# Attention and a long convolution in one kernel: how the convolution's token operand is loaded

## The chip, the cores and the metric

The kernel runs on one core of a Trainium2 chip. The metric is the device time of one execution in microseconds (us). TensorE (PE) multiplies matrices, with its weight loads (PEld) beside them; VectorE (DVE), ScalarE (ACT) and GpSimd (POOL) work on elements; SyncE (SP) issues most of the DMAs. SBUF is the on-chip memory with 128 partitions, PSUM holds TensorE's results.

## What is computed

```python
B, S, D, H = 1, 2048, 448, 16        # Dh = 28, one key and value head
def _A_ref(x, wq, wk, wv, wo):       # attention
    q = (x @ wq).reshape(B, S, H, Dh).transpose(0, 2, 1, 3)
    k = x @ wk
    v = x @ wv
    p = softmax(einsum("bhqd,bkd->bhqk", q, k) * Dh ** -0.5)
    return einsum("bhqk,bkd->bhqd", p, v).transpose(0, 2, 1, 3).reshape(B, S, H * Dh) @ wo

def _B_ref(u, ...):                  # L = 2048 tokens, D = 448 channels, N = 256 modes
    P = exp(logdA[:, :, None] * l)                  # logdA = dt * A, complex
    K = einsum("dn,dnl,dn->dl", Cc, P, dB).real     # one filter of length L for each channel
    y = causal convolution of u with K, by channel  # written with FFTs of length 2 L
    return y + u * Dskip

g = sigmoid((x * gate_w).sum(-1, keepdims=True))
return g * a + (1 - g) * b           # a = _A_ref(x, ...), b = _B_ref(x, ...): u is x too
```

## The kernel before

Everything runs on one core in one program, and a planner orders it. The methods of the class `Kernel` only record operations: an engine, the code that emits the instruction, an estimated duration, the keys that it reads and writes, and a priority `pr`. `Prog.schedule` (a list scheduler, line 186) then goes through them in order of the earliest possible start by its own estimates, with the priority as second criterion, and so fixes one order of instructions for each engine. `emit` writes these orders out with semaphore waits. On the chip nothing is reordered: where an instruction waits longer than the planner thought, all that stands behind it on its engine is late. A DMA is issued from the queue of SyncE, ScalarE or GpSimd, in that engine's order. The planner also puts filler matmuls into gaps of TensorE.

**Attention** (`main`, line 1327). There are 1,024 tiles of 128 keys by 512 queries, in sets of three and two. For each set `qk` puts the scores into five PSUM banks of psS (line 1373 for the form of 29 rows with qT, line 1396 for the form of 128 rows with qM), and one ScalarE instruction takes the exponentials into a ring of 15 tiles, expT (line 1428). `pv` multiplies them with the values into psB (line 1449). After 64 tiles `norm` copies psB to acc (line 1173) on VectorE; the denominators take a round by DRAM (denT, R_scratch, rdenB) on GpSimd's queue. `qproj` makes the next queries (lines 893 to 905), and GpSimd's queue copies them to qM.

**Filters.** `masters` and `tables` build powers of the modes on VectorE (lines 934 to 1024), `kgen` multiplies them into the filters K (line 1047), 32 channels at a time, which go by kstg (line 1059) to the DRAM scratch KP.

**Convolution.** `tload` loads eight channels of K from KP as Toeplitz blocks (tile T, four DMAs on SyncE's queue). Buffers are used in turn: three in T (`NTR`), and late in the program two more in the room of U. `conv` multiplies, for each of 28 groups of 16 channels, with the token operand U as weights and T as the moving operand: for each of four groups of four channels, eight steps `n` of four matmuls that use the four column groups of the array (line 1114). Results go by lines 1124 and 1135 into O (line 1144), which gathers the output and starts as zeros.

**The token operand.** U holds half of the 448 channels (`UA` = 224). Partition 4r + h belongs to row r of a block of 32 tokens and to shift h; on each there are, for every channel, 64 numbers: 16 blocks of tokens for each of four groups i, where group i is zero on partitions with h < i and otherwise the tokens shifted by 512 (h - i). Two channels lie interleaved, so that the columns of one weight load are 4 numbers (8 B) apart. It is made in steps: the DMA zU fills U with zeros; 16 DMAs bring x into O as a staging place; `prep_u` (line 615) moves both halves of the channels with 32-bit copies on VectorE (line 627), the first into U and the second into the tile T at `UB`; 24 DMAs (`ushift`, line 606) copy group 0 with its shifts into the other groups, in pieces of 64 B; the DMA zO then fills O with zeros. Later, when the first half of the channels has been used, `ufill` (line 1091) fills U from T with the second half, seven DMAs for each of seven pieces, on GpSimd's queue.

The loads of this operand may not start before the third store of x (`self.late`). The shifts are written so:

```python
lst.append((bass.AP(tensor=self.U.h, offset=h * rs + do + 32 * i, ap=[[4 * rs, 32], [128, n // 2], [1, 32]]),
            bass.AP(tensor=src.h, offset=(h - i) * src.rs + so, ap=[[4 * src.rs, 32], [sd, n // 2], [1, 32]])))
```

Of the kernel before, what the change touches and what calls it, by code (L numbers as in the profile page):

```python
# [10 lines left out]
BF = mybir.dt.bfloat16  # L11
F32 = mybir.dt.float32
P = 128

S = 2048
D = 448
# [14 lines left out]
MC = 1280  # L31
NTR = 3
RING = 15
# [3 lines left out]
UA = D // 2  # L37
UB = 0
T0 = 16 * (D - UA)
TEND = 17280  # L40
XQ = NT * 512
QS = 4 * D + 64
# [386 lines left out]
class Kernel:  # L429
# [78 lines left out]
    def consts(self):  # L508
# [29 lines left out]
        for k, base in enumerate((-30, -31, -32)):  # L538
            ap = self.sel.v(0, 16, 128 * k, [[32, 4], [1, 32]])
            pm(ap, 1.0, 200, [("sel", k)], 3)  # L540
            pg.op("pool", lambda e, ap=ap, base=base: e.affine_select(
                out=ap, in_=ap, compare_op=ALU.is_equal, fill=0.0, base=base,
                pattern=[[0, 4], [1, 32]], channel_multiplier=2), 300, rd=[("sel", k)], wr=[("sel", k)], pr=3)
        dm(self.one.v(0, P, 0, [[1, 2]]), 1.0, 60, ["one"], 3)
        dm(self.one.v(0, P, 2, [[1, 2]]), 0.0, 60, ["one"], 3)

    def loads(self):
# [12 lines left out]
        def lraw(k, eng="sp"):  # L560
# [27 lines left out]
        Z = lambda n, r: self.cst.v(0, P, 512, [[0, r], [1, n // r]])  # L588
        uc = [("Uc", c) for c in range(14)]
# [15 lines left out]

    def ushift(self, dst, do, src, so, sd, n, r0):
        rs, ts = self.U.rs, self.T.rs
        lst = []
        for i in range(r0, 4):
            for h in range(i, 4):  # L610
                lst.append((bass.AP(tensor=self.U.h, offset=h * rs + do + 32 * i, ap=[[4 * rs, 32], [128, n // 2], [1, 32]]),
                            bass.AP(tensor=src.h, offset=(h - i) * src.rs + so, ap=[[4 * src.rs, 32], [sd, n // 2], [1, 32]])))
        return lst

    def prep_u(self):
        pg = self.pg
        done = []
        U4, T4, O4 = (b.cast(mybir.dt.int32) for b in (self.U, self.T, self.O))
        for half in range(2):
            for k in range(2):  # L620
                if half == 0:
                    dst, w = U4.v(0, P, 8 * k, [[64, UA // 2], [1, 8]]), ["Uz", ("Ub", k)]
                else:
                    dst, w = T4.v(0, P, UB // 2 + 8 * k, [[16, UA // 2], [1, 8]]), ["rawdone", ("UB", k)]
                key = ("ustd", half, k)
                done.append(key)
                pg.op("dve", lambda e, dst=dst, k=k, half=half: e.tensor_copy(
                    dst, O4.v(0, P, (8 * k * D + half * UA) // 2, [[1, UA // 2], [D // 2, 8]])), 1000,
                    rd=[("ust", k)] + ([] if half else []), wr=w + [key], pr=1 + half)
        for k, (c0, c1) in enumerate(((0, 2), (2, 5), (5, 9), (9, 14))):  # L630
            n = 16 * (c1 - c0)
            pg.dma(self.ushift(self.U, 1024 * c0, self.U, 1024 * c0, 128, n, 1), (6 * 16 * n, 64), f"du{k}", rd=[("Ub", 0), ("Ub", 1)],
                   wr=[("Uc", c) for c in range(c0, c1)], pr=0.35 if k < 2 else 0.9 + 0.1 * k, slow=True, iss=700.0)
        V0 = lambda b, off, n, r: b.v(0, P, off, [[n // r, r], [1, n // r]])
        Z = lambda n, r: self.cst.v(0, P, 512, [[0, r], [1, n // r]])
        pg.dma([(V0(self.O, 0, 16 * D, 32), Z(16 * D, 32))], (4096, 448), "zO", rd=[("cst", 1)] + done,
               wr=[(x, q) for q in range(16) for x in ("O", "Oz")], pr=1)

# [429 lines left out]
    def tbufs(self):  # L1068
        home = [(self.T, T0 + k * TW, 0) for k in range(NTR)] + [(self.U, 0, 42), (self.U, TW, 50)]
        last = [-1] * len(home)  # L1070
        self.tb = []
        for gi in range(56):
            s = min((k for k in range(len(home)) if gi >= home[k][2]), key=lambda k: last[k])
            self.tb.append((s, home[s][0], home[s][1], last[s] < 0))
            last[s] = gi

    def tload(self, gi):
        pg = self.pg
        s, buf, o, first = self.tb[gi]
        x = ["tpdone", "rawdone"] + ([("XS", 1)] if gi == NTR - 1 else []) if gi < NTR else []  # L1080
        w = [("T", s)]
        if first and s >= NTR:
            w += [("Uc", k) for k in range(o // 1024, (o + TW - 1) // 1024 + 1)]
# [7 lines left out]
    def ufill(self, c):  # L1091
        pg = self.pg
        lst = [(self.U.v(0, P, c * 2048, [[128, 16], [1, 32]]), self.T.v(0, P, UB + c * 512, [[32, 16], [1, 32]]))]
        lst += self.ushift(self.U, c * 2048, self.T, UB + c * 512, 32, 32, 1)
        for j, pair in enumerate(lst):
            pg.dma([pair], (2048 if j == 0 else 512, 64), f"uf{j % 4}", rd=[("UB", 0), ("UB", 1), ("yx", 2 * c + 5)],
                   wr=[("Uf", 2 * c, j), ("Uf", 2 * c + 1, j)], pr=1.2, slow=True, iss=1800.0 if j == 0 else 800.0, eng="pool", extra=3000)

    def conv(self, c):
# [4 lines left out]
        for k in range(4):  # L1104
# [5 lines left out]
            for n in range(8):  # L1110
                def mm(e, k=k, n=n, to=to, gi=gi, tbuf=tbuf):
                    m0, par = 2 * (n // 2), n % 2
                    for j in range(4):
                        r = e.matmul(ps.v(32 * j, 32 - m0, 128 * k, [[1, 128]]),  # L1114
                                     self.U.v(0, P, (4 * gi + j) % UA // 2 * 128 + 2 * (2 * m0 + par) + j % 2, [[4, 32 - m0]]),
                                     tbuf.v(0, P, to + j * TC + 32 * (13 - 2 * m0 - par), [[1, 128]]),
                                     start=(n == 0), stop=(n == 7), tile_position=(0, 32 * j), skip_group_check=True)
                    return r
                first = k == 0 and n == 0
                o = pg.op("pe", mm, 56, mode="c", ni=8, rd=[("T", s), ("Uc", c % 14), ("Ub", 0), ("Ub", 1)] + [("Uf", c % 14, j) for j in range(7)],  # L1120
                      wr=[X] + ([("cst", cs)] if first else []), pr=1.6,
# [79 lines left out]
    def scaled(self, half):  # L1201
# [4 lines left out]
        ov = self.onT.v(0, P, 512 * 3 + 256 * half, [[1, 256]])  # L1206
        dv = self.seedz.v(0, P, 8 * half, [[1, 8]])
        X, N = ("nx", half), ("dl", half)
# [21 lines left out]
        def m2(e):  # L1230
            for q in range(2):
                for h in range(4):
                    r = e.matmul(gv(32 * h, 32, 128 + 128 * q, [[1, 128]]), self.seedz.v(0, P, 8 * half + 4 * q + h, [[0, 32]]),
                                 self.dg(2 * half + q, [[1, P]]), start=True, stop=True, tile_position=(0, 32 * h), skip_group_check=True)
            return r
# [91 lines left out]
    def main(self):  # L1327
# [159 lines left out]
        for b, (c0, nb) in enumerate(BLOCKS):  # L1487
            self.masters(b)
            for c in range(c0, c0 + nb):
# [3 lines left out]
                self.conv(2 * c + 1)  # L1493
                if 2 <= c < 9:
                    self.ufill(c - 2)
        for a, b in HOLDC:
# [52 lines left out]
```

## Time and profile before

| | |
|---|---|
| three timed runs | 497.27, 497.94, 498.53 us (median 497.94) |
| span of the profiled execution, which is its own time | 498.8 us |
| first exponential starts, last one ends | 21.25 us, 491.98 us |
| busy: PE, DVE, ACT, POOL | 462.3, 458.6, 484.0, 183.8 us |
| granted TensorE clock, mean | 0.997 |
| DMA | 91.86 MB in 117,479 packets, mean 184 GB/s |

All comes from one execution. A group of instructions is named by its line, engine and operation, with the tile that it writes and those that it reads; a number in square brackets is the engine's idle time before it, with the instruction or DMA that ended it. Instructions of an engine overlap a little, so that the sum of their lengths can be more than its busy time.

### The profile page before, as it was taken

Reading aid. Unit: us, or ns where it says so; the run is one execution under the profiler, and the core shown is the slowest. Engines: PE = TensorE matmul, PEld = TensorE weight load, DVE = VectorE, ACT = ScalarE, POOL = GpSimd, SP = SyncE. Lnnn points to the kernel's source line nnn. Section 1 sums busy time; section 2 is a strip of 40 time slices with the busy share of each in tenths; the row PEclk is TensorE's granted clock in tenths of the full one; section 3 lists DMA queues with packets and bytes.
Section 4 is the critical chain, followed back from the end, with each engine's and each line's share of the span. In section 5 each row is a group of like instructions: output and inputs, shape, how many; then the busy total and the mean of one; then the engine's idle time right before and its main releaser. Section 6 shows DMA issues by size and latency. Waiting matters only on the chain.

```text
span 498.8 us, 17277 instructions
## 1 busy us (share of the span) xinstructions
PE 462.3 (93%) x7559; PEld 207.8 (42%) x7645; DVE 458.6 (92%) x872; ACT 484.0 (97%) x436; POOL 183.8 (37%) x331
## 2 busy tenths in 40 slices
PE   8899899999999999999999999999999999999997
PEld 5432233343443444444334344444534344444444
DVE  6998999999999999999999999999999999995224
ACT  6999899999999999999999999999999999999995
POOL 2102034225232527428616552643743525142110
PEclk9999899999999999999999999999999999999999
DMA  8996686935809555776942963798595695877752
GB/s 242 319 187 159 96 174 103 282 119 160 246 12 283 132 184 141 217 205 155 291 124 50 272 171 85 204 234 207 137 279 141 171 285 131 268 207 230 215 175 71
DMA packets 117479, 91.86 MB, mean 184 GB/s; under 512 B 48698, under 2 KB 112492, under 8 KB 117404
## 3 DMA queue, kind: packets, MB, share of 16 engines
q1 hardware_dynamic: 106746, 78.91, 57.7%
q0 software_dynamic: 10384, 11.70, 9.9%
q8 instruction: 60, 0.98, 0.9%
q10 hardware_dynamic: 274, 0.14, 0.1%
q14 instruction: 15, 0.12, 0.1%
HBM read 73.61 MB, written 5.23 MB: 158 GB/s over the span
## 4 chain that ended last, share of the span: by engine, by line
ACT 85%; SPq 6%; PE 4%; DVE 4%; DMA 1%; issue 0%
ACT expT L1428 84%; SPq L164 6%; DVE tab L988 1%; PE psS L658 1%; DMA O<-in_A_x_dram 1%; DVE tab L1003 0%; PE psS L1373 0%; PE psS L1396 0%; PE psS L1286 0%; PE psB L1349 0%; PE psB L1449 0%; ACT L805 0%; PE psS L1047 0%; DVE expT L680 0%; PE psX L1047 0%
## 5 line engine op out<-in xcount | busy, mean ns | idle before, releaser
L1428 ACT ACTIVATE expT<-psS 128x1536 bf16<-128x1536 f32 (+1 forms) x410 | 464.4, 1409 | 3.8 <-PE psS L1373 2.6
L988 DVE TENSOR_TENSOR tab<-tab,mbf 128x512 bf16<-128x512 bf16 (+4 forms) x140 | 139.4, 999 | 0.0
L1373 PE MATMUL psS<-qT,kT 29*128 29x512 bf16 x684 | 96.1, 386 | 12.0 <-ACT expT L1428 6.9
L1449 PE MATMUL psB<-expT,vaug 128*32 128x512 bf16 x1000 | 100.1, 390 | 2.2 <-DVE acc L1173 1.9
L1396 PE MATMUL psS<-qM,kT 128*128 128x512 bf16 x240 | 78.0, 382 | 13.8 <-issue 7.9
L164 POOL DMA_DIRECT2D KP_scratch<-kstg x104 | 57.1, 556 | 65.1 <-DVE kstg L1059 59.5
L1003 DVE TENSOR_TENSOR tab<-tab 128x256 bf16<-128x256 bf16 (+4 forms) x140 | 77.1, 571 | 0.0
L1449 PEld LDWEIGHTS psB<-expT,vaug 128*32 128x32 bf16 x1000 | 25.7, 93 | 74.9 <-issue 70.7
L164 POOL DMA_DIRECT2D qM<-qT x64 | 32.5, 516 | 59.0 <-DVE qT L905 38.4
L1373 PEld LDWEIGHTS psS<-qT,kT 29*128 29x128 bf16 x684 | 23.7, 91 | 64.3 <-ACT expT L1428 50.9
L164 POOL DMA_DIRECT2D U<-T x49 | 36.6, 750 | 36.2 <-DMA U<-T 14.6
L1355 PE MATMUL psB<-ident,one 128*128 128x512 bf16 x149 | 49.0, 389 | 0.0
L164 POOL DMA_DIRECT2D rdenB<-R_scratch x60 | 31.9, 538 | 34.6 <-DMA R_scratch<-denT 33.8
L1114 PE MATMUL psS<-T,U 128*26 128x128 bf16 (+3 forms) x1856 | 42.8, 221 | 0.5 <-issue 0.3
L1114 PEld LDWEIGHTS psS<-T,U 128*26 128x26 bf16 (+3 forms) x1856 | 32.9, 105 | 16.7 <-issue 11.7
L1017 DVE TENSOR_TENSOR tab<-tab,tmp 128x1984 bf16<-128x1984 bf16 x28 | 32.5, 1185 | 0.1
L1114 PE MATMUL psX<-T,U 128*32 128x128 bf16 (+3 forms) x1408 | 31.6, 221 | 0.0
L1396 PEld LDWEIGHTS psS<-qM,kT 128*128 128x128 bf16 x316 | 19.0, 97 | 30.1 <-ACT expT L1428 20.5
L164 POOL DMA_DIRECT2D denT<-acc x15 | 10.7, 716 | 55.8 <-DVE acc L1173 55.8
L1114 PEld LDWEIGHTS psX<-T,U 128*32 128x32 bf16 (+3 forms) x1408 | 24.3, 105 | 11.0 <-issue 7.4
L1011 DVE TENSOR_TENSOR tmp<-tmp,mq 128x64 bf16<-128x64 bf16 (+4 forms) x70 | 25.2, 360 | 0.0
L934 DVE TENSOR_TENSOR msq<-seedz 128x512 f32<-128x512 f32 (+1 forms) x40 | 24.6, 616 | 0.0
(188 smaller groups left out, 502.9 us busy)
## 6 DMA issues: line engine op xcount, KB each, us to landing
T<-KP_scratch SPq DMA_DIRECT2D x204, 272.0 KB, 4.9
U<-KP_scratch SPq DMA_DIRECT2D x20, 272.0 KB, 6.2
rdenB<-R_scratch POOLq DMA_DIRECT2D x60, 64.0 KB, 3.6
U<-cst SPq DMA_DIRECT2D x1, 3584.0 KB, 25.2
qM<-qT POOLq DMA_DIRECT2D x64, 32.0 KB, 3.7
tab<-in_A_x_dram SPq DMA_DIRECT2D x4, 448.0 KB, 5.3
O<-in_A_x_dram SPq DMA_DIRECT2D x16, 112.0 KB, 3.0
O<-cst SPq DMA_DIRECT2D x1, 1792.0 KB, 9.3
```

The source lines that it names most:

```text
L164: return [e.dma_start(o, i, **kw) for o, i in pairs]
L934: pg.op("dve", lambda e: e.tensor_tensor(m2(msq), z2, z2, ALU.mult), el(2 * n), rd=[kr, ki] + first, wr=["msq"], pr=pr)
L988: mul = lambda e, o, a, b: e.tensor_tensor(o, a, b, ALU.mult)
L1003: vo(lambda e, dv=dv, tv=tv, k=k: e.tensor_tensor(dv, dv, tv, ALU.add if k else ALU.subtract), n, [kt[k], kd[k]], [kd[k]], 1.92 if lv else ...
L1011: vo(lambda e, w=w, lv=lv: e.tensor_tensor(rho.v(0, P, (32 - 2 * w) * 2, [[64, 32], [2, w], [1, 2]]), rho.v(0, P, (32 - w) * 2, [[64, 32], ...
L1017: vo(lambda e, k=k: e.tensor_tensor(tab.v(0, P, FM + k * FP + 2, [[64, 32], [2, 31], [1, 2]]), tab.v(0, P, lm + k * PL + 62, [[64, 32], [- ...
L1114: r = e.matmul(ps.v(32 * j, 32 - m0, 128 * k, [[1, 128]]), self.U.v(0, P, (4 * gi + j) % UA // 2 * 128 + 2 * (2 * m0 + par) + j % 2, [[4, ...
L1355: return e.matmul(t.v(0, P, off, [[1, 512]]), self.one.v(0, P, 2, [[0, P]]), self.ident.v(0, P, 0, [[0, 4], [1, P]]), start=b != 6, stop=b ...
L1373: r = e.matmul(self.psS.v(0, P, 512 * b, [[1, 512]]), kT.v(32 * h, DH + 1, 128 * kt, [[1, 128]]), qT.v(32 * h, DH + 1, 512 * (i % 2), [[1, ...
L1396: return e.matmul(self.psS.v(0, P, 512 * b, [[1, 512]]), kT.v(0, P, 128 * kt, [[1, 128]]), self.qM.v(0, P, (i % 2) * XQ + 512 * h, [[1, 51 ...
L1428: o = pg.op("act", lambda e: e.activation(expT.v(0, P, 512 * es[0], spread(es, n)), self.psS.v(0, P, 512 * bs[0], spread(bs, n)), AF.Exp, ...
L1449: r = e.matmul(self.psB.v(32 * h, 32, 0, [[1, 512]]), vaug.v(0, P, 32 * kt, [[1, 32]]), expT.v(0, P, 512 * ring[t], [[1, 512]]), start=(kt ...
```

## The change

U gets another layout: two halves of 112 channels (`UC`), and in each 64 rows of 112 numbers, one for each group and block of tokens. The columns of a weight load are 2 `UC` = 224 numbers (448 B) apart. `uparts` loads every group and shift straight from x in DRAM, in pieces of 224 B: for each of the two halves four DMAs of group 0 and six of groups 1 to 3, on SyncE's queue. The staging in O, the 32-bit copies, the shift copies and the second half in T are gone. U's groups 1 to 3 and O become zero by 20 memsets of GpSimd instead of by DMA. `ufill` loads the second 224 channels from DRAM too, ten DMAs for each of six pieces (`FILLS`), in runs of 64 or 96 B, still on GpSimd's queue. The room that the second half had in T goes to a fourth Toeplitz buffer, and of the two late ones in U one remains. The end of that fourth buffer lies over the first part of the seeds (`seedz`), which moves into T; its first load waits for them.

```diff
-NTR = 3
+NTR = 4
...
-UB = 0
-T0 = 16 * (D - UA)
+UC = UA // 2
+UW = 64 * UC
+T0 = 0
...
+FILLS = ((0, 2), (2, 4), (4, 7), (7, 9), (9, 11), (11, 14))
...
-            self.prep_u()
...
-        self.T = sb("T", TEND, BF)
+        self.T = sb("T", TEND + 4 * W2, BF)
...
-        self.seedz = sb("seedz", 2 * W2, F32)
+        self.seedz = Sub(self.T.cast(F32), TEND // 2)
...
+        U4, O4 = (b.cast(mybir.dt.int32) for b in (self.U, self.O))
+        for b in range(2):
+            for k in range(6):
+                pm(V(U4, (b * UW + 16 * UC) // 2 + 448 * k, 448), 0, 470, [("Uz", b)], 4 + b)
+        for k in range(8):
+            pm(V(O4, 448 * k, 448), 0, 470, [(x, q) for q in (2 * k, 2 * k + 1) for x in ("O", "Oz")], 6)
...
-        self.late.append(pg.dma([(V0(self.U, 0, 64 * UA, 64), Z(64 * UA, 64))], (8192, 448), "zU", rd=[("cst", 1)],
-                                wr=["Uz"], pr=0.25).i)
-        for k in range(2):
-            lst = [(self.O.v(0, P, (8 * k + j) * D, [[1, D]]),
-                    dram(x, 32 * (15 - 8 * k - j) * D, [[D, 32], [512 * D, 4], [1, D]])) for j in range(8)]
-            self.late.append(pg.dma(lst, (1024, 896), f"u{k}", wr=[("ust", k)], pr=0.3).i)
+        self.x = x
+        for b in range(2):
+            for k, i0 in ((0, 0), (1, 1)):
+                lst = self.uparts(UC * b, UC * b, UC, (0, 1) if k == 0 else (1, 4))
+                o = pg.dma(lst, (512 * len(lst), 2 * UC), f"u{b}{k}", rd=[("Uz", b)] if k else [],
+                           wr=[("Uc", c) for c in range(7 * b, 7 * b + 7)] if k else [("Ub", b)], pr=0.3 + 0.6 * b)
+                self.late.append(o.i)
...
+    def uparts(self, dc, sc, n, groups):
+        rs = self.U.rs
         lst = []
+        for i in range(*groups):
             for h in range(i, 4):
+                lst.append((bass.AP(tensor=self.U.h, offset=h * rs + dc // UC * UW + 16 * i * UC + dc % UC,
+                                    ap=[[4 * rs, 32], [UC, 16], [1, n]]),
+                            dram(self.x, (512 * (h - i) + 480) * D + sc, [[D, 32], [-32 * D, 16], [1, n]])))
         return lst
...
-        home = [(self.T, T0 + k * TW, 0) for k in range(NTR)] + [(self.U, 0, 42), (self.U, TW, 50)]
+        home = [(self.T, T0 + k * TW, 0) for k in range(NTR)] + [(self.U, 0, 42)]
...
-        w = [("T", s)]
+        w = [("T", s)] + ([("zr", 0)] if first and o + TW > TEND else [])
...
+    def ufill(self, k):
         pg = self.pg
+        c0, c1 = FILLS[k]
+        n = 16 * (c1 - c0)
+        for j, pair in enumerate(self.uparts(16 * c0, UA + 16 * c0, n, (0, 4))):
+            pg.dma([pair], (512, 2 * n), f"uf{j % 4}", rd=[("yx", c1 + 3)],
+                   wr=[("Uf", c, j) for c in range(c0, c1)], pr=1.2, iss=800.0, eng="pool", extra=3000)
...
-                                     self.U.v(0, P, (4 * gi + j) % UA // 2 * 128 + 2 * (2 * m0 + par) + j % 2, [[4, 32 - m0]]),
+                                     self.U.v(0, P, (4 * gi + j) % UA // UC * UW + (2 * m0 + par) * UC + (4 * gi + j) % UC, [[2 * UC, 32 - m0]]),
```

More of the change, by code (lines that the diff above doesn't have):

```diff
@@ L615, in prep_u @@
[L615 to L637, printed above, removed]
@@ L1080, in tload @@
         x = ["tpdone", "rawdone"] + ([("XS", 1)] if gi == NTR - 1 else []) if gi < NTR else []
-        w = [("T", s)]
+        w = [("T", s)] + ([("zr", 0)] if first and o + TW > TEND else [])
         if first and s >= NTR:
-            w += [("Uc", k) for k in range(o // 1024, (o + TW - 1) // 1024 + 1)]
+            w += [("Uc", k) for k in range(7)]
         rs = buf.rs
@@ L1119, in conv @@
                 first = k == 0 and n == 0
-                o = pg.op("pe", mm, 56, mode="c", ni=8, rd=[("T", s), ("Uc", c % 14), ("Ub", 0), ("Ub", 1)] + [("Uf", c % 14, j) for j in range(7)],
+                o = pg.op("pe", mm, 56, mode="c", ni=8, rd=[("T", s), ("Uc", c % 14), ("Ub", c % 14 // 7)] + [("Uf", c % 14, j) for j in range(10)],
                       wr=[X] + ([("cst", cs)] if first else []), pr=1.6,
@@ L1232, in m2 @@
                 for h in range(4):
[L1233 removed]
+                    r = e.matmul(gv(32 * h, 32, 128 + 128 * q, [[1, 128]]), self.seedz.v(0, P, 576 + 8 * half + 4 * q + h, [[0, 32]]),
                                  self.dg(2 * half + q, [[1, P]]), start=True, stop=True, tile_position=(0, 32 * h), skip_group_check=True)
@@ L1493, in main @@
                 self.conv(2 * c + 1)
-                if 2 <= c < 9:
-                    self.ufill(c - 2)
+                for k, (c0, c1) in enumerate(FILLS):
+                    if (c1 + 3) // 2 == c:
+                        self.ufill(k)
         for a, b in HOLDC:
```

14 lines of the change are left out of this document (1 added, 13 removed).

## The prediction

> **What bounds the kernel now.** The profile page comes first: its engine shares, its chain and its costliest group.
>
> ```profile
> PE 462.3 (93%) x7559; PEld 207.8 (42%) x7645; DVE 458.6 (92%) x872; ACT 484.0 (97%) x436; POOL 183.8 (37%) x331
> ...
> ACT 85%; SPq 6%; PE 4%; DVE 4%; DMA 1%; issue 0%
> ...
> L1428 ACT ACTIVATE expT<-psS 128x1536 bf16<-128x1536 f32 (+1 forms) x410 | 464.4, 1409 | 3.8 <-PE psS L1373 2.6
> ```
>
> ScalarE is busy for 484.0 of 498.8 us, and 464.4 of these are the 410 exponentials of attention. Before them it stood idle for 3.8 us in all. So the time can change in three places only: before the first exponential (21.25 us), in these 3.8 us, or after the last (491.98 to 498.8). ScalarE's timeline shows where most of the 3.8 us lie. Columns: start, length, group, idle time before it.
>
> ```profile
> 59.45 1.02 ACT L1428 ACTIVATE expT<-psS 128x1024 bf16<-128x1024 f32 x1 [0.95 <-PE psS L1373]
> 61.51 2.52 ACT L1428 ACTIVATE expT<-psS 128x1536 bf16<-128x1536 f32 x2 [1.03 <-PE psS L1373]
> 64.39 4.62 ACT L1428 ACTIVATE expT<-psS 128x1536 bf16<-128x1536 f32 x4 [0.36 <-PE psS L1373]
> 69.25 11.40 ACT L1428 ACTIVATE expT<-psS 128x1536 bf16<-128x1536 f32 x10 [0.23 <-PE psS L1373]
> 80.92 411.06 ACT L1428 ACTIVATE expT<-psS 128x1536 bf16<-128x1536 f32 x364 [0.26 <-PE psB L1449]
> ```
>
> From 80.92 us on, 364 exponentials run for 411.06 us without a gap that counts. The convolution fills all of that stretch and delays nothing in it. Between 59 and 70 us ScalarE loses 0.95 + 1.03 + 0.36 + 0.23 = 2.57 us. Why TensorE was late there is read backwards, in its own timeline, then in VectorE's, then in the chain of waits.
>
> ```profile
> 58.69 0.40 PE L1449 MATMUL psB<-expT,vaug 128*32 128x512 bf16 x4 [1.94 <-DVE acc L1173]
> ```
>
> ```profile
> 50.92 0.95 DVE L627 COPY U<-O 128x896 int32<-128x896 int32 x1 [2.99 <-DMA O<-in_A_x_dram]
> 51.78 0.95 DVE L627 COPY T<-O 128x896 int32<-128x896 int32 x1
> ...
> 57.93 0.70 DVE L1173 COPY acc<-psB 128x512 f32<-128x512 f32 x1
> ```
>
> ```profile
> 17.11 20.72 SPq L164
> ...
> 48.03 2.87 DMA O<-in_A_x_dram
> ```
>
> One staging load stuck in SyncE's queue for 20.72 us behind the 3.5 MB of zeros for U. The last one landed at 50.9 us. VectorE, whose order is fixed, stood 2.99 us in front of a 32-bit copy of it. Everything behind the copy came later, also the copy that frees psB (line 1173). The next values' matmul waited 1.94 us for that, and the score matmuls queued behind it on TensorE reached ScalarE late. After this VectorE hardly waits until 455 us (from 81 to 455 it is busy for 371.7 of 374.0 us).
>
> **The change, part by part.** The sum is made against the profiled span, 498.8 us. The median of the timed runs, 497.94, is 0.86 lower, and I carry this difference over.
>
> *Staging removed.* Gone are 16 loads into O, the zero fills of U and O, 24 shift DMAs and four 32-bit copies. The four copies are 3.8 us of VectorE's work, and the wait 2.99 us more. VectorE is not what ends the program (it rests after 455 us), so the work itself earns nothing. The wait does: the 2.57 us of ScalarE go with it, since nothing on VectorE depends on the token rows any longer. Bounds: 0 (the planner's new order brings a like wait) to 2.83 (the 0.26 at 80.92 goes too). I take 2.57, because VectorE shows no other wait on a load between 6 and 455 us. What would be late next is the small loss at 80.92, where table matmuls stand between score matmuls.
>
> *Token rows loaded from DRAM.* SyncE issues 20 DMAs where it issued 42, at about 0.6 us each. Behind them stand Wo, the Dskip row and the Toeplitz loads. The first Toeplitz load leaves at 83.98, so all this is covered by some 50 us. The data is 10,240 pieces of 224 B. A 224 B piece takes 26 ns in this trace (median of the 112 on that queue), so 10,240 x 26 / 16 = 16.6 us of all 16 DMA engines, from 15.4 to about 32 us. The fill with zeros and the staging loads kept the engines as full in those microseconds. The first qM transfers are issued at 21.0 to 22.7 us there, and the slowest takes 8.05 us, to 30.7. That is what the first matmul from qM waits for (30.83), and ScalarE loses 0.72 us at 31.7. I leave this at 0. Bounds: 0.72 gained (qM lands as at 40.5 us, in 2.3 to 2.6 us) to 2 us lost (a quarter longer to land).
>
> *Zeros by GpSimd.* Twenty memsets of 448 elements are added.
>
> ```profile
> 0.81 0.20 POOL L511 MEMSET ident<- 128x128 bf16 x1 [0.29 <-POOLq L1534]
> 1.08 0.20 POOL L511 MEMSET expT<- 128x128 bf16 x1
> ...
> 2.48 0.09 POOL L511 MEMSET expT<- 28x1 bf16 x1
> ...
> 73.23 2.72 POOL L164 DMA_DIRECT2D rdenB<-R_scratch x4 [3.51 <-DMA R_scratch<-denT]
> ...
> 103.97 1.98 POOL L164 DMA_DIRECT2D rdenB<-R_scratch x4 [3.45 <-DMA R_scratch<-denT]
> ```
>
> One element takes 0.09 us and 128 take 0.20, so 448 take 0.09 + 447 x 0.11 / 127 = 0.48, and about 0.07 lies between two. Twenty are 11 us. GpSimd rests from 4.75 to 21.03 us, so they end near 16 and no DMA of its queue waits. The six that the first loads need end by 8. The cost lies elsewhere. Four rdenB issues took 2.72 us beside VectorE's short copy (line 1021) and scaling (line 1024), and 1.98 at another time. So the two engines disturb each other, and from 10 to 21 us VectorE is on the path to the first exponential. Its exposed kinds there are the 0.63 us scaling (line 831), the 0.62 us copy of Wq and two copies of 0.18. If two of them wait half a memset each, that is 0.48. Bounds 0 and 4 x 0.48 = 1.9. I take 0.3, nearer to the lower end, since the trace shows GpSimd as the one that waits. The Trainium skill's "SBUF — State Buffer", section "Who interferes with whom", says that one port pair is held for a whole instruction by whichever of the two engines starts first. By that VectorE could lose as well; only the GpSimd side shows in this trace.
>
> *Weights with a stride.* The convolution's weight columns stood 8 B apart and now stand 448 B apart.
>
> ```profile
> L1114 PEld LDWEIGHTS psS<-T,U 128*32 128x32 bf16 x464 | 11.4, 109 | 5.5 <-issue 3.2 <-DVE tab L1024 0.4
> ```
>
> The first matmul of a burst lasts 247 ns and the following ones 219, so 28 ns of a 32-column load are exposed. Later loads hide behind steps of four matmuls that start 56 ns apart (486.553, .609, .665 us). The load must therefore more than double before the step grows. No row has such a stride. Bounds: 0, and the price in the first rival. I take 0, with 64 bursts (254 of the 3,584 matmuls last over 240 ns, four to a burst) that start up to 28 ns later, 1.8 us of TensorE beside its 58 us of waiting for ScalarE in the long stretch.
>
> *Refills and buffers.* The refills go from 49 to 60 DMAs on GpSimd's queue. At the 0.66 us of the smaller ones that is 39.6 us against 36.6, and GpSimd is busy 37%. Behind them stand the K writes, qM and the denominators' transfers, which VectorE's reciprocals and SyncE's Toeplitz loads wait for. These have not held VectorE up so far, so 0, priced below. The fourth Toeplitz buffer earns nothing, since those loads wait for K rather than for a buffer:
>
> ```profile
> SPq L164 <- DMA KP_scratch<-kstg: 102.5, 12, 19.5
> ...
> SPq L164 <- PE psS L1114: 25.0, 7, 11.6
> ```
>
> *Sum.* 498.8 - 2.57 + 0.3 = 496.5 us of span, and 0.86 less for the median: **495.6 us**. A measurement of this kernel tells about 0.3% (1.5 us) from no change.
>
> **The rivals.** *The load outgrows its step (slower).* This is one mechanism, at the convolution's weight loads. A burst has 896 / 64 = 14 steps. TensorE's two score groups wait 58 us for ScalarE in 166 waits from 81 to 492 us, so 0.35 us covers a burst. A load of 84 ns (three times) adds 14 x 28 ns = 0.39 us to each: 64 x 0.04 = 2.6 us over, 498.2. It is slower than before from there on. Four times (112 ns) adds 0.78: 64 x 0.43 = 28 us, 523. For it: no operand here is read so widely apart. Against it: today's 28 ns leaves a factor of two. The Trainium skill's "SBUF — State Buffer", section "Door 1: The DMA port swizzle", speaks against the change: reads are at full rate only with two or more hits in a 16-byte line, which 8 B gives and 448 B does not. It names no size for the penalty, and no run so far shows one.
>
> *GpSimd's queue falls behind (slower).* Ten refills on four slots wait twice for a landing where seven waited once. The longest such wait was 4.3 us. If six refills each hold VectorE 1 us beyond its cover, ScalarE loses about 2.57 / 2.99 of it as at 59 us: 6 x 0.86 = 5.2, 500.8. For it: 14.6 us of such waits now. Against it: VectorE did not notice them.
>
> *The gain is not there.* The planner orders all operations anew, and a like stall appears between 45 and 80 us, or qM and the memsets take it back: 495.6 + 2.57 = 498.2 at most, 497 if half. For it: the lost 0.72 and 0.26 show how small a misfit suffices. Against it: over those 374 us the fixed orders of VectorE and ScalarE never lost step.
>
> **How the numbers follow.** Forecast 0.56, no gain 0.20, GpSimd's queue 0.13, the weight loads 0.11. Faster by over 0.3% (under 496.4) is the forecast's 0.56; within 0.3% is 0.20; slower is the other two, 0.24. The forecast's own range is 494 (qM's 0.72 and the 0.26 gone too, and the memsets free) to 496.4. The whole range goes up to 500.5, which leaves out the upper part of the slower cases.
>
> **What would show it.** Right: no VectorE wait on a load between 40 and 60 us, no ScalarE idle time over 0.3 us between 55 and 75, a first exponential at 21.2 to 21.6, and about 411 us without a gap after it. The weight loads should last up to 28 ns longer and the steps stay at 56 ns. Wrong: steps over 56 ns with ScalarE waiting all along for line 1373; VectorE waiting for denT; the first exponential past 22.5; or a new wait for qM at 31 us.

## The result and the profile after

The changed kernel took 500.75 us (median of 500.34, 500.49, 501.0 and 502.06), the kernel before 497.75 us (four runs, 497.27 to 498.53). The ratio is 1.0062, with a 95% interval of 1.0042 to 1.0082: slower by about 3 us, where 495.6 was forecast. Comparisons below are ratios to the kernel before, run on the same chip each time. The profiled execution of the changed kernel is the run of 500.49 us; its span is 498.7 us.

The page's lines for the shares, the chain and the exponentials:

```profile
PE 478.2 (96%) x7643; PEld 217.7 (44%) x7643; DVE 456.0 (91%) x868; ACT 484.6 (97%) x436; POOL 197.5 (40%) x362
...
ACT 77%; PE 15%; DMA 2%; SPq 0%; issue 0%
...
L1412 ACT ACTIVATE expT<-psS 128x1536 bf16<-128x1536 f32 (+1 forms) x410 | 464.8, 1363 | 3.5 <-PE psS L1357 1.4
```

ScalarE still bounds the kernel, and in total it idles before the exponentials about as long as in the profile of before (3.5 for 3.8 us). But the idle time is elsewhere, as ScalarE's timeline shows (start, length, group, idle time before it):

```profile
21.71 1.45 ACT L1412 ACTIVATE expT<-psS 128x1536 bf16<-128x1536 f32 x1
...
66.20 6.88 ACT L1412 ACTIVATE expT<-psS 128x1536 bf16<-128x1536 f32 x6 [0.23 <-PE psS L1357]
74.19 253.32 ACT L1412 ACTIVATE expT<-psS 128x1536 bf16<-128x1536 f32 x224 [1.11 <-PE psB L1433]
328.28 141.80 ACT L1412 ACTIVATE expT<-psS 128x1536 bf16<-128x1536 f32 x125 [0.77 <-PE psS L1357]
470.71 1.02 ACT L1412 ACTIVATE expT<-psS 128x1024 bf16<-128x1024 f32 x1 [0.63 <-PE psS L1380]
```

The stalls at 59 to 70 us are gone but for 0.23, as forecast, and so is the one at 31.7. New are a first exponential 0.46 us later, 1.11 us at 74, 0.77 at 328 and, with two small ones behind it, 1.02 at 470 to 477. The last exponential ends at 492.41 and the span 6.3 us later (6.8 in before).

TensorE's 478.2 us are not 16 us more work than the 462.3 of before. That profile lacks rows (7,559 matmuls to 7,645 weight loads); two later profiles of the same kernel (e1_before and e10_before_third_look below), with 7,645 of each, show 475.8 and 477.0 us.

The rows behind the terms of the sum: the VectorE copies on the path to the first exponential with the memsets that run beside them, SyncE's issues of the operand, the weight loads (busy, mean ns), and GpSimd's waits for the refills (total, times, longest).

```profile
14.51 0.95 DVE L588 COPY Wq<-mbf 112x1792 bf16<-112x1792 bf16 x1
15.38 0.67 DVE L680 TENSOR_REDUCE small<-kT 128x1 f32<-128x512 bf16 x1
15.97 0.47 DVE L590 COPY expT<-seedw 112x112 bf16<-112x112 bf16 x1
16.07 0.40 DVE L592 COPY expT<-seedw 112x4 bf16<-112x4 bf16 x1
```

```profile
5.34 5.57 POOL L512 MEMSET U<- 128x448 int32 x10
...
12.03 4.37 POOL L512 MEMSET O<- 128x448 int32 x7
```

```profile
15.26 24.52 SPq L166 DMA_DIRECT2D U<-in_A_x_dram  x20
```

```profile
L1098 PEld LDWEIGHTS psS<-T,U 128*26 128x26 bf16 (+3 forms) x1792 | 35.7, 138 | 14.9 <-issue 10.2
```

```profile
POOL U L166 <- DMA U<-in_A_x_dram: 10.3, 9, 3.7
```

### The profile page after: what moved, and what is told of

It is laid out like the page before. It is cut to its first block, busy times and chain, and to the rows that moved or that the text cites. A ratio compares the mean times of both kernels' runs of the same rounds, so it can differ in the third digit from the quotient of the medians.

```text
span 498.7 us, 17357 instructions
## 1 busy us (share of the span) xinstructions
PE 478.2 (96%) x7643; PEld 217.7 (44%) x7643; DVE 456.0 (91%) x868; ACT 484.6 (97%) x436; POOL 197.5 (40%) x362
## 4 chain that ended last, share of the span: by engine, by line
ACT 77%; PE 15%; DMA 2%; SPq 0%; issue 0%
ACT expT L1412 77%; PE psS L1380 2%; PE psS L1357 2%; PE psB L1433 2%; DMA T<-KP_scratch 2%; PE psX L1098 1%; PE psS L1098 1%; PE psS L1031 1%; PE psB L1333 1%; PE psS L1368 1%; PE psS L1242 0%; PE psB L1427 0%; SPq L166 0%; PE psX L1031 0%; PE psX L1119 0%; PE psB L1339 0%
## 5 line engine op out<-in xcount | busy, mean ns | idle before, releaser
L1380 PE MATMUL psS<-qM,kT 128*128 128x512 bf16 x316 | 95.1, 383 | 0.8
L166 POOL DMA_DIRECT2D KP_scratch<-kstg x104 | 58.1, 565 | 75.5 <-DVE kstg L1043 74.0
L166 POOL DMA_DIRECT2D U<-in_A_x_dram x60 | 39.9, 669 | 25.0 <-DMA U<-in_A_x_dram 10.3
L1339 PE MATMUL psB<-ident,one 128*128 128x512 bf16 x146 | 47.2, 384 | 0.0
L1098 PEld LDWEIGHTS psS<-T,U 128*26 128x26 bf16 (+3 forms) x1792 | 35.7, 138 | 14.9 <-issue 10.2
L1098 PE MATMUL psS<-T,U 128*26 128x128 bf16 (+3 forms) x1792 | 41.0, 226 | 1.1 <-DMA T<-KP_scratch 1.1
L1098 PE MATMUL psX<-T,U 128*26 128x128 bf16 (+3 forms) x1600 | 38.9, 227 | 0.7 <-issue 0.7
L1098 PEld LDWEIGHTS psX<-T,U 128*26 128x26 bf16 (+3 forms) x1600 | 32.6, 139 | 11.9 <-issue 9.5
L918 DVE TENSOR_TENSOR msq<-T 128x512 f32<-128x512 f32 (+1 forms) x40 | 24.6, 616 | 0.0
```

Of the source, the lines that this page charges most:

```text
L166: return [e.dma_start(o, i, **kw) for o, i in pairs]
L918: pg.op("dve", lambda e: e.tensor_tensor(m2(msq), z2, z2, ALU.mult), el(2 * n), rd=[kr, ki] + first, wr=["msq"], pr=pr)
L1098: r = e.matmul(ps.v(32 * j, 32 - m0, 128 * k, [[1, 128]]), self.U.v(0, P, (4 * gi + j) % UA // UC * UW + (2 * m0 + par) * UC + (4 * gi + j ...
L1339: return e.matmul(t.v(0, P, off, [[1, 512]]), self.one.v(0, P, 2, [[0, P]]), self.ident.v(0, P, 0, [[0, 4], [1, P]]), start=b != 6, stop=b ...
L1380: return e.matmul(self.psS.v(0, P, 512 * b, [[1, 512]]), kT.v(0, P, 128 * kt, [[1, 128]]), self.qM.v(0, P, (i % 2) * XQ + 512 * h, [[1, 51 ...
```

## The experiments

Kernels built on the changed one with the zeros moved (e2, e5, e6, e9, e11, e12) have line numbers four higher than it.

**What the kernel before does in other executions** (e1_before, e10_before_third_look: no edit).

> The kernel before, unchanged, for a second profile of it. The question is whether the 2.57 us that ScalarE lost at 59 to 70 us, behind VectorE's 2.99 us wait for the last staging load, is there in an ordinary execution. The changed kernel's runs are 1.7 to 1.8 us longer than their spans. If that holds for the kernel before, its median of 497.75 us means a span near 496.0 and its profile (498.8) was a long one. Theory A (the stall is not usual): span 495.5 to 496.8, VectorE's wait at its line 627 under 1 us, ScalarE's idle time between 59 and 70 us under 0.8 us. Theory B (the stall is always there): span near 498.8, the wait near 3 us, the idle time near 2.6 us, and the two kernels would differ in what lies around the span.

Measured: 497.69 us, ratio 1.0002 (0.9987 to 1.0016); the profiled run took 496.71 us with a span of 494.9, a little under the 495.5 expected. ScalarE's timeline and VectorE's first staging copy that waits:

```profile
33.16 31.97 ACT L1428 ACTIVATE expT<-psS 128x1536 bf16<-128x1536 f32 x28 [0.16 <-PE psS L1396]
65.36 11.40 ACT L1428 ACTIVATE expT<-psS 128x1536 bf16<-128x1536 f32 x10 [0.23 <-PE psS L1373]
77.03 411.06 ACT L1428 ACTIVATE expT<-psS 128x1536 bf16<-128x1536 f32 x364 [0.26 <-PE psB L1449]
```

```profile
47.89 0.94 DVE L627 COPY U<-O 128x896 int32<-128x896 int32 x1 [0.48 <-DMA O<-in_A_x_dram]
```

> The kernel before, once more, for its profile alone. Theory A (VectorE's long wait for the last staging load and the 2.57 us of ScalarE stalls at 59 to 70 us belong to single executions): no ScalarE stall over 0.3 at 55 to 72 us, VectorE's wait for that load under 1.0. Rival B (they are there in about every second execution, and the span of 494.9 was a lucky one): stalls of 1.5 to 3 us there and a span of 497 or more.

Measured: 499.06 us, span 497.3. VectorE's wait is above the 1.0 expected, and the stall isn't there.

```profile
49.51 0.95 DVE L627 COPY U<-O 128x896 int32<-128x896 int32 x1 [1.23 <-DMA O<-in_A_x_dram]
```

```profile
66.66 11.40 ACT L1428 ACTIVATE expT<-psS 128x1536 bf16<-128x1536 f32 x10 [0.23 <-PE psS L1373]
78.33 390.23 ACT L1428 ACTIVATE expT<-psS 128x1536 bf16<-128x1536 f32 x345 [0.26 <-PE psB L1449]
468.97 5.63 ACT L1428 ACTIVATE expT<-psS 128x1024 bf16<-128x1024 f32 x5 [0.41 <-PE psS L1396]
475.03 15.50 ACT L1428 ACTIVATE expT<-psS 128x1536 bf16<-128x1536 f32 x14 [0.43 <-PE psS L1373]
```

VectorE's wait for the last staging load is 2.99, 0.48 and 1.23 us in three executions of the same program. Only the first reaches ScalarE. In the other two the stretch that I wanted to shorten by 2.57 us holds 0.23, and the changed kernel has the same 0.23. The longest of these three spans is the one that I worked from. In all 100 executions of this kernel whose span is listed, the time is 1.69 to 1.87 us above the span, so by estimate a span of 498.8 belongs to about 500.5 us. Of the 89 that ran beside the experiments, 75 lie between 497.0 and 498.8, with a median of 497.73, and two lie above 500.

The profile of before holds something else in that stretch that I had passed over: TensorE's granted clock, the third number from the end of the first row (before it stand the stretch, its length and the busy time of each engine). The rows behind it are TensorE's.

```profile
60.00:63.00 3.00, 3.00 (x15) 0.60 (x14) 3.00 (x5) 1.92 (x2) 0.00 (x0) 0.50 0.90 164
```

```profile
59.34 1.58 PE L1355 MATMUL psB<-ident,one 128*128 128x512 bf16 x4
60.85 0.61 PE L1373 MATMUL psS<-qT,kT 29*128 29x512 bf16 x3
...
63.95 0.39 PE L1373 MATMUL psS<-qT,kT 29*128 29x512 bf16 x3
```

From 59.7 to 63.1 us the clock was halved: three score matmuls took 0.61 us there, and 0.39 behind it. So VectorE's wait explains the first loss, 0.95 us, directly. Of the 1.03 us that followed, about 0.8 are the slower matmuls (an estimate: four warm-ups took 1.58 us, where three at 55.6 us took 0.82 and four would take 1.03, and the scores 0.61 instead of 0.39). Neither of the other two profiles of before has such a stretch ahead of its end. Four profiles here have one, each 3.41 us long: this one, e3 from 176.2 us, e4 from 226.0 and e11 from 290.7. In the 3.41 us ahead of each, TensorE had been idle for 1.1 to 2.3 us (1.94 in before, the wait for acc). But in e8 it was idle for 1.42 us out of 3.41 (up to 475.2 us) and nothing followed; what sets such a stretch off was not tested.

One of these stretches takes 3.41 x 0.5 / 498 = 0.0034 off the mean clock, so the mean clocks on record tell which executions had one (0.997 or less): 3 of the 100 of before, and 22 of the 27 of the changed kernel and the three variants that keep its order (e3, e7, e8). The changed kernel's profile, at 0.999, is one without.

The last profile of before also loses 0.84 us at 467 to 475 us. TensorE's rows there show idle time that no semaphore ended, as do the profiles of the changed kernel (e7 below):

```profile
468.09 0.30 PE L1114 MATMUL psX<-U 128*30 128x128 bf16 x6 [0.80 <-issue]
474.42 0.24 PE L1114 MATMUL psS<-T,U 128*26 128x128 bf16 x1 [0.59 <-issue]
```

**The zeros late** (e2_late_zeros): the 20 memsets wait for the first qM transfer.

```diff
+            if i == 0:
+                for z in self.zs:
+                    pg.after[z] = pg.ops[-1].i
```

> The changed kernel with its 20 memsets of GpSimd placed behind the first qM transfers (about 23 us) instead of from 4.4 to 16 us. The first exponential started at 21.71 us in the changed kernel and at 21.25 in the one before; VectorE's copy of Wq took 0.95 us instead of 0.62, two small copies 0.47 and 0.40 instead of 0.18. Theory A (GpSimd's memsets hold VectorE up on the way to the first exponential): it starts at 21.25 +- 0.1 us, Wq's copy is back to 0.62, and the time falls by 0.4 to 0.5 us to about 500.3. Theory B (the start is late for another reason, such as the changed load order): still 21.7, time unchanged within 0.2 us.

Measured: 499.97 us, ratio 1.0043 (1.0031 to 1.0055). VectorE's timeline:

```profile
14.27 0.62 DVE L589 COPY Wq<-mbf 112x1792 bf16<-112x1792 bf16 x1
14.80 0.68 DVE L681 TENSOR_REDUCE small<-kT 128x1 f32<-128x512 bf16 x1
15.40 0.18 DVE L591 COPY expT<-seedw 112x112 bf16<-112x112 bf16 x1
15.49 0.17 DVE L593 COPY expT<-seedw 112x4 bf16<-112x4 bf16 x1
```

The copies are back at their 0.62, 0.18 and 0.17 us (0.95, 0.47 and 0.40 beside the memsets), while the reduction lasts the same in both. From ScalarE's exponential of the time steps (line 788 in the changed kernel) to the first exponential of attention it is 16.24 us here and 16.68 in the changed kernel. Of the nine profiles without early memsets seven show 16.20 to 16.24, and two are late without them (e12 16.46, e10 16.76); the other four with early memsets show 16.49 to 16.98. So the memsets cost 0.3 to 0.5 us, once 0.8. The median fell by 0.78, more than that; 3 of these 7 executions have a mean clock of 0.997, against 3 of the changed kernel's 4. The Trainium skill's "SBUF — State Buffer", section "Who interferes with whom", says that copies can contend for the pair that VectorE shares with GpSimd, and that reductions never do: both agree with these rows.

**Weight columns 8 B apart again** (e3_weights_8B): the loads read other data, from Wo, in the old spacing; the token operand is left out of the convolution.

```diff
-   self.U.v(0, P, (4 * gi + j) % UA // UC * UW + (2 * m0 + par) * UC + (4 * gi + j) % UC, [[2 * UC, 32 - m0]]),
+   self.Wo.v(0, P, 128 * ((4 * gi + j) % 8) + 2 * (2 * m0 + par) + j % 2, [[4, 32 - m0]]),
```

> The changed kernel with the convolution's weights read from Wo with columns 8 B apart instead of from U 448 B apart. It leaves out the token operand: the convolution's numbers are of other weights; count, shapes, waits and order stay. Theory A (the distance of the columns lengthens the loads, 138 ns against 104, and steps, 62.6 ns on average against 57.8, which costs ScalarE the 1.0 us at 470 to 477 us and some 0.5 us in small pieces): loads back at about 104 ns, those losses gone, time 1.0 to 1.6 us lower, near 499.4. Theory B (the whole loss against the kernel before comes from the strided weights, since TensorE is busy for 478 us against 462): about 3 us lower, 497.8. Theory C (the distance costs the end nothing): unchanged within 0.3 us although the loads shorten.

Measured: 500.9 us, ratio 1.0059 (1.0037 to 1.008). The group of weight loads:

```profile
L1098 PEld LDWEIGHTS psS<-T,Wo 128*26 128x26 bf16 (+3 forms) x1792 | 30.5, 105 | 14.6 <-issue 10.2 <-DVE mbf L938 0.4
```

A load takes 105 for 138 ns, and a step of four matmuls 57.8 for about 62 ns in the mean (56 for 57 in the median). The end does not move. By estimate, 896 steps x 4.4 ns, the wide spacing costs TensorE 4 us; it costs ScalarE nothing that these runs resolve. (All four executions here have a half-clock stretch, which took 1.18 us from ScalarE in the profile; so have three of the changed kernel's four.)

**Three Toeplitz buffers** (e4_three_buffers): `NTR = 3` for 4 in the changed kernel, so one late buffer in U and three in T.

> The changed kernel with three Toeplitz buffers in T instead of four, and the one late buffer in U. My prediction said the fourth earns nothing, since loads wait for K and not for a buffer. If so: time within 0.5 us of the changed kernel's 500.75. The rival: the fourth buffer stands in for the second late one in U, which the new layout has no room for, and at the end of the program, where four to five buffers are in use, a missing one delays the last convolutions: 2 to 6 us longer, with ScalarE or the tail waiting after 440 us.

Measured: 510.15 us, ratio 1.0256 (1.0219 to 1.0293). ScalarE's timeline and TensorE's at the two largest stalls:

```profile
226.46 1.02 ACT L1412 ACTIVATE expT<-psS 128x1024 bf16<-128x1024 f32 x1 [2.06 <-PE psS L1380]
228.80 248.27 ACT L1412 ACTIVATE expT<-psS 128x1536 bf16<-128x1536 f32 x219 [1.32 <-PE psS L1357]
```

```profile
225.47 0.29 PE L1098 MATMUL psX<-T,U 128*32 128x128 bf16 x4 [2.30 <-DMA T<-KP_scratch]
```

The load behind this wait left at 215.83 us and took 9.59 us to land, beside seven refills that GpSimd issued from 212.9 to 220.4. With four buffers the same load, the twentieth group of four, left at 208.34 us. The 1.32 us lie in the half-clock stretch that followed the wait (226.0 to 229.4 us). Two stalls of 1.06 and 0.93 near the end and an end of 10.9 us behind the last exponential make the rest. The fourth buffer is what lets the loads leave early enough. It earns over 9 us, the slower clock included: all four executions have a mean of 0.987 to 0.996. The largest stalls come long before the 440 us that the rival named.

**No refills** (e8_no_refills): `ufill` issues nothing, so the later channels use the first ones' tokens.

> The changed kernel without its 60 refill loads of the token operand (60 of the loads from the input behind the first 20): the later channels' convolution reads the first channels' tokens. Theory A (what the prediction said: the refills cost the end nothing, the loss is in order and start): the time stays within 0.5 of the changed kernel's 500.75. Rival B (the refills fill the DMA queues and hold the Toeplitz loads back, median landing 5.6 against 4.9 us before): T's landing falls to 5.0 or less, no stall at T, and the time falls by 0.8 to 1.5, to 499.3 to 500.

Measured: 500.66 us, ratio 1.0057 (1.0033 to 1.0082). T's median landing is 5.3 us (5.6 with the refills), and the time is that of the changed kernel. With four buffers the refills cost nothing that shows (each interval is about 1 us to either side). The 0.77 us at 328 us, where a Toeplitz load landed late, is in none of the other profiles of this order; it belongs to one execution.

**The filters behind the warm-ups** (e5_filters_after_warmups): e2, and one priority. TensorE's order in the changed kernel ahead of the stall at 74 us:

```profile
68.36 0.40 PE L1433 MATMUL psB<-expT,vaug 128*32 128x512 bf16 x4
68.69 0.43 PE L1031 MATMUL psX<-tab 128*64 128x128 bf16 x8
...
71.63 0.89 PE L1031 MATMUL psS<-tab 128*64 128x128 bf16 x24
72.45 0.39 PE L1357 MATMUL psS<-qT,kT 29*128 29x512 bf16 x3
72.78 0.60 PE L1333 MATMUL psB<-ident,cst 128*128 128x512 bf16 x2
73.22 0.59 PE L1380 MATMUL psS<-qM,kT 128*128 128x512 bf16 x2
73.74 0.40 PE L1433 MATMUL psB<-expT,vaug 128*32 128x512 bf16 x4
```

For 5.4 us no values' matmul (line 1433) runs, so no tile of the ring comes free. The 64 filter matmuls (line 1031) go ahead of two warm-ups (line 1333), and values stand behind warm-ups because both write psB. VectorE has no staging copies any longer, so these filters start at 68.7 us, where e1_before has them at 72.8.

```diff
-                          wr=[(X, q), ("kst", q)], pr=1.15, lock=G if k == 0 else None)
+                          wr=[(X, q), ("kst", q)], pr=1.15 if c else 1.97, lock=G if k == 0 else None)
```

> The changed kernel with the zeros late (as in e2) and the filter matmuls of the first 32 channels given priority number 1.97 in the planner, behind the warm-up matmuls' 1.95; all other filters stay at 1.15. Theory A (the stall at 74 us comes from the order: with VectorE's staging copies gone the first filter matmuls are ready 6 us sooner, go ahead of two warm-up matmuls, and value matmuls of the same accumulation bank stand behind those warm-ups): the ScalarE stall of 1.09 at 73.7 us in e2 falls under 0.3, and the median is 0.8 to 1.0 below e2's 499.97, about 499.0. Rival B (TensorE simply has too much work in these microseconds, the order only says where it shows): a stall of the same 0.8 to 1.1 in all appears between 70 and 82 us, and the time stays at 500.0. The stall of 1.02 at 470 us is expected to be there still, at another place within 465 to 480 us perhaps.

Measured: 499.3 us, ratio 1.0023 (1.0004 to 1.0042). ScalarE runs from 65.69 to 473.31 us without a gap that counts; the next stall, 1.06 us, is at 474. The stall at 74 was the order, and nothing took its place. (In e1_before values pause for 5.7 us at 71 to 77 as well and ScalarE loses only 0.26. What made that pause cheaper was not tested.)

**Forty instructions more ahead** (e7_shifted_instructions): the changed kernel, with two narrow matmuls at each of the first ten warm-ups.

```diff
         def warm(e):
+            if type(e).__name__ != "E" and self.nx < 10:
+                self.nx += 1
+                for _ in range(2):
+                    e.matmul(self.psB.v(0, P, 0, [[1, 16]]), self.cst.v(0, P, 512, [[1, P]]), self.ident.v(0, P, 0, [[1, 16]]),
+                             start=False, stop=False, tile_position=(0, 0), skip_group_check=True)
```

> The changed kernel in its own order, with 20 narrow matmuls (16 columns, adding zero) more on TensorE, two at each of the first ten warm-ups, that the planner doesn't know of: the order of all else is the same, and everything behind them is 40 instructions further on in the stream. Theory A (TensorE's idle time at 469.00 to 469.69 in the middle of a convolution burst is the end of a block of 256 instructions whose successor hasn't come): the idle time moves 20 matmuls forward in the order, out of the burst behind the value matmuls into the one before it, and other idle times of 0.3 to 1 us without a semaphore may come up at other blocks, since the planner's accounts are off by 40; time 500.5 to 503. Rival B (a bank conflict, a late semaphore or the Toeplitz loads): the idle time stays at the 13th matmul of the same burst, time 500.5 to 501.2.

Measured: 502.51 us, ratio 1.0093 (1.0063 to 1.0123). TensorE's timeline around the idle time, first of the changed kernel, then of this one:

```profile
467.73 0.39 PE L1339 MATMUL psB<-ident,one 128*128 128x512 bf16 x1
468.05 0.39 PE L1357 MATMUL psS<-qT,kT 29*128 29x512 bf16 x3
468.37 0.40 PE L1433 MATMUL psB<-expT,vaug 128*32 128x512 bf16 x4
468.60 0.40 PE L1098 MATMUL psX<-T,U 128*26 128x128 bf16 x13
469.69 0.44 PE L1098 MATMUL psX<-T,U 128*30 128x128 bf16 x15 [0.69 <-issue]
```

```profile
467.70 0.39 PE L1346 MATMUL psB<-ident,one 128*128 128x512 bf16 x1
468.53 0.39 PE L1364 MATMUL psS<-qT,kT 29*128 29x512 bf16 x3 [0.44 <-issue]
468.86 0.40 PE L1440 MATMUL psB<-expT,vaug 128*32 128x512 bf16 x4
469.08 0.59 PE L1098 MATMUL psX<-T,U 128*26 128x128 bf16 x28
```

The gap stood behind 3 + 4 + 13 = 20 matmuls, and now stands ahead of them: exactly the 20 matmuls (40 instructions with their weight loads) that were added. No data or semaphore moves by that count. Two longer gaps of the same kind, 1.21 us at 457.6 and 0.93 at 473.4, cost ScalarE 1.08 and 0.99 us. The three gaps of this profile lie 254 and 127 matmuls apart; in the changed kernel a second gap, 0.21 us at 475.8, comes 127 matmuls behind the first, and the two of before's last profile are 126 apart. With their weight loads, 127 matmuls are 254 instructions. So TensorE stood at the end of a block of instructions whose successor had not come. In the profile the 60 transfers of the instruction queue q8 carry 0.98 MB, 16 KB each, for 15,286 TensorE instructions: 255 to a transfer. The Trainium skill's "Runtime: NRT & Kernel Launch", section "Instruction fetch mechanics", gives the same block of 256. It says that the fetch is hidden, and that the cost at a block's end mostly is; in these gaps it isn't.

**More time for the fetch** (e6_other_fetch_spacing, and e12_e6_again, the same kernel): e5, and the planner lets filling work reach the next block 0.4 us later from 440 us on.

```diff
-  else self.FETCH if r < self.QUIET else self.IDLE))
+  else self.FETCH + (400.0 if r > 440000.0 else 0.0) if r < self.QUIET else self.IDLE))
```

> As e5, and the planner lets TensorE's filling work reach the next 256 instructions 0.4 us later from 440 us on (5.2 for 4.8 us between two instruction transfers), which changes the order there. Theory A (the stall of 1.0 at 470 us is TensorE waiting for an instruction transfer that came late): no ScalarE stall over 0.6 between 440 and 480 us, and the median 0.8 to 1.0 below e5's, near 498.0, the time of before. Rival B (it is something else that the order doesn't touch, or the transfer is later still): a stall of 0.6 to 1.1 stays there and the time equals e5's within 0.3.

> e6 unchanged, for comparison on the same chip as e11 and as a second measurement of the order without stalls. Theory A (with the three order stalls gone the layout is worth nothing either way): within 0.3% of before again, 497.7 to 498.7, no ScalarE stall over 0.3 between 70 and 485 us. Rival B (the missing stall at 470 us was luck of one profile): a stall of 0.5 to 1.1 us at 465 to 480 us is there this time.

Measured: 498.14 us, ratio 1.0003 (0.9985 to 1.0022), and again 498.01 us, ratio 1.0004 (0.9992 to 1.0016). ScalarE's timeline of the first:

```profile
65.33 422.96 ACT L1416 ACTIVATE expT<-psS 128x1536 bf16<-128x1536 f32 x374 [0.23 <-PE psS L1361]
```

From 65 us on all 374 exponentials run without a gap that counts, in both profiles, and none of these 23 executions has a half-clock stretch (mean clock 0.999 or more; e5's twelve have none either). The time is that of before.

**A shorter reach and another end** (e9_shorter_window: 0.3 us, from 440 to 472 us only; e11_other_tail: e6 with the planner's `NEED` 0.020 for 0.015 and `HOLDC` empty).

> As e6, but the later reach of TensorE's filling work holds only from 440 to 472 us and by 0.3 us (5.1 for 4.8), so that the work behind the last exponential isn't held back: in e6 the span ends 7.7 us behind the last exponential, in the changed kernel 6.3. Theory A (what is left of e6's distance to a faster kernel is this end): no ScalarE stall over 0.6 at 440 to 480 us, an end of 6.3 to 6.9, and a median 0.5 to 1.3 below e6's 498.14, thus 496.8 to 497.6, at or just under the time of before. Rival B (0.3 is not enough, the stall for the instruction transfer is back): a stall of 0.5 to 1.1 there, 498.0 to 499.0.

> As e6, with two more planner settings changed to bring the last convolution's back-transform before the last exponential again: NEED 0.020 for 0.015 (filling work spread more evenly over a block of 256 instructions) and HOLDC empty (the convolution of channel group 24 no longer held behind the last filter). Theory A (the layout itself costs nothing any more, and e6's end of 7.7 us is what keeps it from being faster): the end behind the last exponential is 6.3 to 6.9 and the median 0.8 to 1.5 below e6's of this batch. Rival B (the other order brings its own stall of 0.5 to 1.1 us somewhere, as every order so far but e6's did): time between e6's and 0.8 above it.

Measured: e9 took 498.69 us, ratio 1.0020 (1.0007 to 1.0033). Its end is still 7.6 us, and gaps of 0.37 and 0.56 us without a semaphore are back on TensorE at 468 and 473 us. The time is the rival's; ScalarE loses only 0.29 and 0.17 us behind them, less than the 0.5 that the rival named. e11 took 497.53 us, ratio 1.0000 (0.9987 to 1.0012), 0.48 below e12 on the same chip, less than the 0.8 expected; its end is 6.4 us, but a stall of 0.76 us is new at 293, in a half-clock stretch (290.7 to 294.1 us). Six of its twelve executions have such a stretch; their median is 498.2 us, that of the other six 497.1. No version beat the kernel before.

## Why the prediction was wrong, point by point

- **The 498.8 us and the 2.57 us.** This is the step that failed: *Staging removed* takes 2.57 us off a span of 498.8, but that execution was a rare one. Ordinary executions of before have a span of about 497.73 - 1.75 = 496.0 us and 0.23 of the 2.57. Even for the profiled one the chain from SyncE's queue to ScalarE is only half of it: VectorE's wait cost 0.95 us directly, the 1.03 and 0.36 came while TensorE ran at half clock and shortly after, which the chain leaves out, and the last 0.23 is in every profile. The -0.86 that I carried over already said that the profile was slower than the timed runs. I took it for a fixed offset, and it has the wrong sign: the time is 1.75 above the span. The rival on GpSimd's queue was priced with the same stall (2.57 / 2.99).
- **"The planner's new order brings a like wait."** I gave it a bound of 0 to the term and 0.20 as a case. It happened, without the gain that it should have eaten: 1.11 us at 74 us, and about 1.0 at 470 to 477. I looked only for VectorE and loads as causes; the causes were TensorE's own order and its instruction blocks. The second is not the new order's alone, since one of three profiles of before has it too. The ratios go down step by step: 1.0062 as changed, 1.0043 without the early memsets, 1.0023 with the filters moved too, 1.0003 with the fetch as well. The intervals of neighbours overlap, so each single step of about 0.2% rests on the trace (its stall is there or gone) as much as on the times. Nor is each step one cause alone: the half-clock stretches, in 3 of 4, 3 of 7 and none of 12 executions, went with the first two. Why the changed order has them so often stays open.
- **The memsets, 0.3.** Right in mechanism and place, 0.3 to 0.5 us measured. VectorE did lose as well, which the trace of before had not shown.
- **qM.** The 0.72 at 31.7 us did go, but e1_before lacks it too and e10_before_third_look has 0.41, so the change can be given little of it.
- **The weight loads, 0.** Right for the end. The load grew by 33 ns, against 28 forecast as its limit, and the steps grew from 57.8 to about 62 ns in the mean, where I had said that they stay at 56. That a load must more than double before its step grows was wrong: a third more was enough. The cover of TensorE's waits took the 4 us.
- **The refills, 0.** Right as far as e8 can tell.
- **"The fourth Toeplitz buffer earns nothing."** Wrong: without it 510.15 us. I compared it with three buffers before, but the change also takes one of the two late ones in U, and the waits for K told only how the loads wait while buffers suffice.
- **The rivals.** The time came out where two rivals put it, slower, but by neither of their mechanisms; 0.24 had been given to that side. 500.75 lies 0.25 above the range, whose upper end was 500.5. Of the signs that I named, the VectorE wait is gone as said, but the first exponential (21.71 us) and the idle time at 74 us are not as said, and none of the four signs of being wrong came up.

## What to carry to other kernels

Before costing the removal of a stall, ask whether it belongs to the program or to one execution: set the profile's own time (its span and what lies around it) against the timed runs, and where it is the slowest of them, doubt the stall first. Read the granted clock of the very stretch too: a mean of 0.997 over the program hid 3.4 us at half speed in the stall that I wanted to remove. In a program whose order is planned ahead, an edit that removes work from a waiting engine changes every order behind it. Price that new order as a term of its own, and look in it for operations that write one bank in a fixed sequence and for where the instruction blocks end.

## What the hardware showed that was not expected

- TensorE waits for its own instructions. Gaps of 0.4 to 1.4 us without a semaphore came up at 457 to 477 us, 126, 127 or 254 matmuls apart where a profile has several, and shifted with the count of instructions (e7).
- TensorE's granted clock fell to 0.50 for 3.41 us in the middle of four profiles, each time behind 3.41 us in which TensorE had been idle for 1.1 to 2.3 us, in one piece or several.
- Three VectorE copies beside GpSimd memsets of 0.48 us lasted 0.23 to 0.33 us longer each, while a reduction between them did not.
- A weight load of 26 to 32 columns that lie 448 B apart takes 138 ns, against 105 ns for 8 B.
